# Identity matmuls placed in the planned waits of TensorE, in the attention stage of a fused attention and mixture-of-experts kernel

## The chip, the cores and the metric

The kernel runs on one core of one Trainium2 chip. The metric is the device time of one execution in microseconds (us). Lower is better. The time before is 783.3 us, the median of 3 runs (781.61 to 784.54).

## What is computed

The reference is attention with rotated queries and keys, and behind it a mixture of eight experts of which each token takes two.

```python
# q, k, v: (4, 8, 576, 64) float32
q_rot, k_rot = rotate(q), rotate(k)
scores = q_rot @ k_rot.T / sqrt(64)
attn = exp(scores - max(scores)); attn /= sum(attn) + 1e-9
x = (attn @ v)                       # as rows: (2304, 512)
noisy = x @ w_gate + log1p(exp(x @ w_noise)) * noise
top2_w = softmax of the two largest of noisy
out[token] += top2_w * (relu(x @ w1[e]) @ w2[e])   # for the two experts e of the token
```

## The kernel before

The kernel has two stages. Attention runs until about 350 us and handles 32 heads as 16 pairs. The experts run from about 356 us to the end. Between them the tokens are routed: logits, places and indirect DMAs that put each token's row into its experts' lists.

In attention each pair has nine score blocks in two passes. Pass 1 (`s1`, with keys as the moving operand) computes the scores for the row maxima. VectorE (DVE) reduces each block (`mx`, L556). Pass 2 (`s2`) computes the scores again, transposed, and takes the maximum off by a further matmul with `qlm`. ScalarE (ACT) takes the exponential (`ex`, L656), and the result is split in two 16-bit parts by DVE (L663), GpSimd (POOL, L667) or ACT (L660). Both passes contract over 64 rows, so that they use half of TensorE's rows at a time (64-row form). Then `av` multiplies the probabilities with the values and sums them up in `ACC` (128-row form).

`ACC` is one tile of PSUM with two banks of 512 columns, one for each head of the pair. The sums use columns 0 to 324 of each bank. There is one `ACC` for all pairs. When the last `av` of a pair is done, DVE normalises the sums in place (`n0` to `n2`, L751), ACT copies them out (`xh`, L772) and DVE takes the remainder out (`xl`, L770). Only then can the first `av` of the next pair write to `ACC`. The score blocks go through a ring of three other PSUM tiles (`ps`, two banks each, named `big`).

All of this is laid out by a planner within the kernel's source (`Plan`). Every step is an `Op` with an engine, a planned duration, its dependencies, a priority and the buffers that it uses. `Plan.order()` plays the steps through with these durations, and gives each one a planned begin and end. The steps are then issued in the order of their planned begins, engine by engine, and this order is fixed: an instruction that has to wait on the chip holds whatever stands behind it on its engine. TensorE (PE) and the others find each other by semaphores that the framework sets where two instructions touch the same tile; in PSUM it orders any two that touch the same bank. The planner adds `SWITCH` (.095 us) where TensorE goes from the 64-row to the 128-row form or back.

At the start, `warm` issues 24 matmuls of a 128x128 identity (`ident`) into columns 0 to 127 of `ACC` (L863). Four groups of transposes follow (L443, 5 matmuls each), and later 5 transposes of the maxima (L598). `swap_left` is the point in the plan at which attention's buffers are given up.

Of the kernel before, what the change touches and what calls it, by code (L numbers as in the profile page):

```python
# [22 lines left out]
NP = B * H // 2  # L23
# [9 lines left out]
FAR = 1 << 20  # L33

SWITCH = .095
LAG = dict(PE=.16, DVE=.05, ACT=.05, POOL=.05, SP=.05, Z=0.0)
CFG = {'T': 12.38,
 'bufP': 5,
# [116 lines left out]
class Ring:  # L155


    def __init__(self, name, bufs, make):
        self.name, self.bufs, self.make, self.taken = name, bufs, make, []


class Buf:


    def __init__(self, ring, make=None):
        self.ring, self.make, self.left, self.t, self.held = ring, make or ring.make, 0, None, False

    def __call__(self):
        if self.t is None:
            self.t = self.make()  # L170
        return self.t
# [9 lines left out]
class Plan:  # L181
# [14 lines left out]
    def order(self):  # L196
        for op in self.ops:
            for d in set(op.deps):
                p = self.by[d]
                p.out.append(op)  # L200
                op.left += 1
        now, k, port, rows = 0.0, 0, None, 128
        ready = {e: [] for e in ("PE", "DVE", "ACT", "POOL", "SP", "Z")}
        run, ev, dma, started = {}, [], 0.0, []

        def push(t, kind, op):
            nonlocal k
            k += 1
            heapq.heappush(ev, (t, k, kind, op))

        for op in self.ops:
            if op.after > 0:
                op.left += 1
                push(op.after, "start", op)
            if op.left == 0:
                ready[op.eng].append(op)

        def free(op):
            for b in op.uses:
                if b.held:  # L220
                    continue
                n = len(b.ring.taken)
                if n >= b.ring.bufs and b.ring.taken[n - b.ring.bufs].left:
                    return False
            return True

        def reach(op, same):
            for q in op.out:
                if (q.eng == op.eng and op.land is None) == same:
                    q.left -= 1  # L230
                    if q.left == 0:
                        q.rdy = now
                        ready[q.eng].append(q)

        def go():
            nonlocal port, rows
            any_ = True
            while any_:
                any_ = False
                for e, rl in ready.items():  # L240
                    if e in run or not rl:
                        continue
                    for op in sorted(rl, key=lambda o: o.prio):
                        if free(op):
                            break
                    else:
                        continue
                    rl.remove(op)
                    for b in op.uses:
                        if not b.held:  # L250
                            b.held = True
                            b.ring.taken.append(b)
                    op.begin = now
                    started.append(op)
                    run[e] = [op, op.dur]
                    if e == "PE":
                        run[e][1] += SWITCH if op.rows != rows else 0.0
                        rows = op.rows
                    any_ = True
                    if op.port and port is None:  # L260
                        port = e
                    if e == "Z":
                        finish(e)

        def finish(e):
            nonlocal dma, port
            op = run.pop(e)[0]
            op.end = now
            if port == e:
                port = next((x for x, r in run.items() if r[0].port), None)  # L270
            if op.land is not None:
                dma = max(dma, now + 0.3) + op.land
                push(dma + 1.4, "far", op)
            else:
                push(now + LAG[e], "far", op)
                reach(op, True)

        while True:
            go()
            on = [e for e, r in run.items() if not r[0].port or e == port]  # L280
            t = min([now + run[e][1] for e in on] + ([ev[0][0]] if ev else []), default=None)
            if t is None:
                break
            for e in on:
                run[e][1] -= t - now
            now = max(now, t)
            for e in [e for e, r in run.items() if r[1] < 1e-9]:
                finish(e)
            while ev and ev[0][0] <= now + 1e-9:
                _, _, kind, op = heapq.heappop(ev)  # L290
                if kind == "start":
                    op.left -= 1
                    if op.left == 0:
                        op.rdy = now
                        ready[op.eng].append(op)
                else:
                    reach(op, False)
                    for b in op.uses:
                        b.left -= 1
        stuck = [o.name for o in self.ops if o.begin is None]  # L300
        assert not stuck, (len(stuck), now, stuck[:40])
        self.span = now
        return started


def build(ctx, tc, q, k, v, w_gate, w_noise, noise, w1, w2, tab_d, out):
    nc = tc.nc
# [13 lines left out]
    plan = Plan()  # L321
# [7 lines left out]
    ACC = sml.tile([128, 2, 512], F32, name="acc")  # L329
# [8 lines left out]
    ident = cp.tile([128, 128], F16, name="ident")  # L338
# [13 lines left out]
    bigs = Ring("big", 3, lambda: big.tile([128, 1024], F32, name="ps"))  # L352
# [430 lines left out]
    def simple(name, eng, dur, fn, prio=-95.0, deps=(), **kw):  # L783
        add(name, eng, dur, fn, deps=deps, prio=prio, **kw)
# [73 lines left out]
        simple(("zero", i), "ACT", .6, lambda i=i: fill_out(i), prio=210 + 7 * i, land=1.4,  # L858
               deps=["pad"], after=210 + 7 * i)

    def warm(n):
        for _ in range(n):
            nc.tensor.matmul(ACC[:, 0, 0:128], ident, ident, start=True, stop=True)  # L863
    simple("warm", "PE", 2.4, lambda: warm(24), prio=-99, deps=["ident", ("add", "q", 0, 0)])


# [511 lines left out]
    for o, d in zip(plan.ops, CFG["dp"].split()):  # L1378
        o.prio += int(d) / 10
    todo = plan.order()  # L1380
    if CFG.get("dry"):
        return plan, todo
    for o in todo:
        for b in o.uses:
            b()
        o.fn()
    manual.close()

# [107 lines left out]
```

## Time and profile before

| what | value |
|---|---|
| median of 3 runs | 783.3 us (781.61 to 784.54) |
| profiled execution, its own time | 784.09 us |
| span of that execution, first to last instruction | 782.3 us |
| granted TensorE clock, mean over the span | 0.969 |
| TensorE (matmul) busy | 714.0 us, 91% |
| DVE, ACT, POOL busy | 410.9, 284.3, 363.5 us |

The span is what the trace shows; 1.8 us of the execution lie outside it. A granted clock of 1.00 is 2.4 GHz and 0.50 is 1.2 GHz. "Idle before" is the time in which an engine had nothing running just before an instruction, with what ended it. Matmuls are pipelined: one that takes 219 ns from start to end can start 58 ns behind the one before it.

### The profile page before, as it was taken

What the parts mean: (1) busy time and instruction counts of PE and PEld (TensorE: products, weight loads), DVE (VectorE), ACT (ScalarE), POOL (GpSimd) and SP (SyncE); (2) the same over time, 40 slices, a digit from 0 to 9 for tenths busy, and PEclk for the clock granted to TensorE, in tenths of its full rate; (3) what the DMA queues carried; (4) which work ended last, traced back from release to release, by engine and by line L of the source; (5) the groups of instructions that cost most, each with busy time, mean ns of one, the idle gap of its engine ahead of it and who ended that gap; (6) DMA issues with size and microseconds to landing.
All of it is one profiled execution on the core that took longest, in us unless ns stands there. A gap on an engine that the chain in (4) does not pass through costs nothing.

```text
span 782.3 us, 17906 instructions
## 1 busy us (share of the span) xinstructions
PE 714.0 (91%) x7736; PEld 484.7 (62%) x7736; DVE 410.9 (53%) x653; ACT 284.3 (36%) x428; POOL 363.5 (46%) x315
## 2 busy tenths in 40 slices
PE   3889878989897889889999999999999999999995
PEld 2667666777775767778655557456465574664652
DVE  6758768867858868668224515334333343342211
ACT  2543637535545555845113313213223132140100
POOL 4699797894523678744622313131330321312311
PEclk9989989989898999999999999999999999999998
DMA  7675756957726595566755697745555437441201
GB/s 154 146 155 119 144 116 140 194 90 117 131 56 147 199 177 173 148 166 214 243 153 161 124 165 204 203 128 150 175 165 163 132 114 202 129 134 54 78 28 39
DMA packets 178808, 112.09 MB, mean 143 GB/s; under 512 B 150431, under 2 KB 155039, under 8 KB 178720
## 3 DMA queue, kind: packets, MB, share of 16 engines
q1 hardware_dynamic: 161632, 72.72, 42.5%
q0 software_dynamic: 9120, 29.03, 11.0%
q10 hardware_dynamic: 7968, 9.12, 3.5%
q8 instruction: 62, 1.02, 0.5%
q14 instruction: 26, 0.21, 0.1%
HBM read 58.57 MB, written 29.22 MB: 112 GB/s over the span
## 4 chain that ended last, share of the span: by engine, by line
PE 50%; issue 12%; DVE 6%; DMA 6%; POOL 5%; ACT 3%; POOLq 0%; ACTq 0%; DVEq 0%
PE ps L531 24%; PE dn L531 18%; PE acc L531 7%; DMA prev<-out_dram,meta 3%; DMA out_dram<-y,meta 2%; POOL p L667 2%; POOL out_dram L1296 1%; POOL prev L1250 1%; DVE xr L770 1%; ACT p L656 1%; ACT xr L772 1%; DMA qlm<-tmx 1%; DVE acc L751 1%; ACT ps L656 1%; DVE nm L556 1%
## 5 line engine op out<-in xcount | busy, mean ns | idle before, releaser
L531 PE MATMUL dn<-w2h,hid 128*128 128x512 f16 x640 | 192.0, 379 | 0.0
L531 PE MATMUL ps<-xt,w1h 128*128 128x320 f16 (+2 forms) x960 | 177.6, 301 | 0.2 <-DVE hid L1223 0.2
L1296 POOL DMA_INDIRECT out_dram<-y,meta x40 | 53.3, 1332 | 247.8 <-DVE y L1289 204.0
L531 PEld LDWEIGHTS <-hid 128*128 128x128 f16 x960 | 93.9, 98 | 111.7
L667 POOL TENSOR_TENSOR p<-p 128x1152 f16<-128x1152 f32 (+1 forms) x50 | 102.4, 2060 | 61.2 <-ACT p L656 60.8
L531 PEld LDWEIGHTS <-w1h 128*128 128x128 f16 x1024 | 100.0, 98 | 41.6 <-issue 0.9
L1225 ACT ACTIVATE hid<-ps 128x640 f16<-128x640 f32 (+2 forms) x80 | 47.8, 597 | 210.9 <-PE ps L531 210.9
L531 PE MATMUL dn<-w2l,hid 128*128 128x512 f16 x320 | 121.3, 379 | 0.0
L531 PE MATMUL ps<-xt,w1l 128*128 128x320 f16 (+2 forms) x480 | 113.1, 301 | 0.0
L656 ACT ACTIVATE p<-ps,pbias 128x576 f32<-128x576 f32 x115 | 81.5, 741 | 84.6 <-PE ps L531 79.4
L556 DVE TENSOR_REDUCE nm<-ps 128x2 f32<-128x576 f32 x128 | 91.7, 751 | 33.3 <-PE ps L531 32.9
L1223 DVE SCALAR_TENSOR_TENSOR hid<-ps,hid 128x640 f16<-128x640 f32 (+2 forms) x80 | 54.8, 690 | 99.1 <-ACT hid L1225 99.1
L531 PE MATMUL ps<-qt,kt 64*128 64x288 f16 (+5 forms) x1200 | 88.4, 270 | 15.3 <-DVE p L663 4.6
L1289 DVE SCALAR_TENSOR_TENSOR y<-dn,gsc,prev 128x512 f32<-128x512 f32 x38 | 28.5, 751 | 139.9 <-PE dn L531 120.6
L531 PE MATMUL acc<-vb,p 128*128 128x65 f16 (+3 forms) x2040 | 81.7, 197 | 12.0 <-DVE xr L770 5.8
L531 PE MATMUL ps<-kt,qt 64*128 64x288 f16 (+1 forms) x960 | 83.9, 302 | 6.4 <-DVE nm L556 2.6
L531 PEld LDWEIGHTS <-p 128*128 128x128 bf16 (+3 forms) x2040 | 72.8, 100 | 26.5 <-issue 16.2
L531 PEld LDWEIGHTS <-kt 64*128 64x128 f16 (+1 forms) x1200 | 56.1, 100 | 30.6 <-issue 22.5
L531 PEld LDWEIGHTS <-qt 64*128 64x128 f16 (+1 forms) x960 | 49.1, 101 | 24.7 <-issue 14.1
L1250 POOL DMA_INDIRECT prev<-out_dram,meta x38 | 41.9, 1101 | 46.9 <-DMA out_dram<-y,meta 28.2
L531 PEld LDWEIGHTS <-w1l 128*128 128x128 f16 x512 | 50.1, 98 | 19.4
L1058 POOL DMA_INDIRECT xs_rows<-xr,r_ii x36 | 41.7, 1158 | 30.6 <-DVE r_got L1046 12.6
(136 smaller groups left out, 747.8 us busy)
## 6 DMA issues: line engine op xcount, KB each, us to landing
wst<-in_moe_w_dram SPq DMA_DIRECT2D x64, 512.0 KB, 4.2
out_dram<-pad ACTq DMA_DIRECT2D x18, 256.0 KB, 3.9
xs_rows<-pad ACTq DMA_DIRECT2D x8, 522.0 KB, 3.3
qin<-in_q_dram SPq DMA_DIRECT2D x16, 256.0 KB, 4.1
qin<-in_k_dram SPq DMA_DIRECT2D x16, 256.0 KB, 3.8
vin<-in_v_dram SPq DMA_DIRECT2D x16, 256.0 KB, 3.5
out_dram<-y,meta POOLq DMA_INDIRECT x40, 5.0
prev<-out_dram,meta POOLq DMA_INDIRECT x38, 3.8
```

What stands on the lines that cost most here:

```text
L531: nc.tensor.matmul(o, w, m, start=first, stop=last, skip_group_check=True)
L556: nc.vector.tensor_reduce(nm()[:, u, :, h], x, axis=AX.X, op=OP.max, negate=True)
L656: nc.scalar.activation(x if way[u] == "P" else halves(whole(u), u, h), x, AF.Exp, bias=pbias, scale=0.125 / (QS * QS))
L667: E.tensor_tensor(b, whole(u), a, op=OP.subtract)
L751: nc.vector.tensor_tensor(xv(), a5[:, :, :, 0:64], ri[0][:, :, :, None].to_broadcast([128, 2, 5, 64]), op=OP.mult)
L770: nc.vector.tensor_tensor(at_, xx, to, op=OP.subtract)
L1058: i = nc.gpsimd.indirect_dma_start(out=xs, out_offset=bass.IndirectOffsetOnAxis(ap=h["ii"][:, t, a:a + 1], axis=0), in_=r[:, slot(t)], in_ ...
L1223: nc.vector.scalar_tensor_tensor(hl, ps[:, 0:n, 0:w_], 0.0, hh, op0=OP.max, op1=OP.subtract)
L1225: nc.scalar.activation(hh, ps[:, 0:n, 0:w_], AF.Relu)
L1250: nc.gpsimd.indirect_dma_start(out=prev, out_offset=None, in_=out, in_offset=bass.IndirectOffsetOnAxis(ap=ids(e, j, 1), axis=0))
L1289: nc.vector.scalar_tensor_tensor(y, dn(), s["gsc"][j], s["prev"][j], op0=OP.mult, op1=OP.add)
L1296: i = nc.gpsimd.indirect_dma_start(out=out, out_offset=bass.IndirectOffsetOnAxis(ap=ids(e, j, 0), axis=0), in_=yt[0], in_offset=None, boun ...
```

## The change

TensorE gets extra matmuls of the identity with itself ("fills"), whose results nobody reads. After the planner has ordered all steps, a new passage looks at each pair of PE steps that follow each other in the plan, up to `swap_left`. A planned wait gets fills in front of the step `z` that ends it, if it is at least .3 us long, begins after `warm`, and if the planned busy share of PE is at most `LOW` (.8) in at least one of three stretches of 3.4 us around it. Their number is `FILL` (.7) of the wait less .1 us, divided by .055 us.

Where they write is chosen as follows. If the wait does not overlap a planned reading of `ACC` (from the begin of a pair's last `av` to .2 us after its last `xl`), they go to columns 384 to 511 of `ACC`'s first bank, without the start flag. Otherwise, if `z` is a score block whose `ps` tile is planned to be free by the start of the wait, they go to columns 320 to 447 of that tile, with the start flag. Otherwise there are none. `Buf` and `Plan` only note when a buffer was done with; the order of the steps is that of before. `warm` itself moves from columns 0 to 127 to columns 384 to 511.

```diff
+LOW, FILL = .8, .7
...
         self.ring, self.make, self.left, self.t, self.held = ring, make or ring.make, 0, None, False
+        self.since = self.done = 0.0
...
                             b.held = True
+                            if len(b.ring.taken) >= b.ring.bufs:
+                                b.since = b.ring.taken[-b.ring.bufs].done
                             b.ring.taken.append(b)
...
                     for b in op.uses:
                         b.left -= 1
+                        b.done = now
...
-    def warm(n):
+    def warm(n, to=None, begin=True):
         for _ in range(n):
-            nc.tensor.matmul(ACC[:, 0, 0:128], ident, ident, start=True, stop=True)
+            nc.tensor.matmul(ACC[:, 0, 384:512] if to is None else to[:, 320:448], ident, ident, start=begin, stop=True,
+                             skip_group_check=True)
...
     todo = plan.order()
+    busy = [o for o in todo if o.eng == "PE" and o.begin < plan.by["swap_left"].begin]
+    reads = [(min(plan.by["av", n, 8, j].begin for j in range(2)), max(plan.by["xl", n, m].end for m in range(2)) + .2)
+             for n in range(NP)]
+
+    def share(a, z):
+        return sum(max(0.0, min(z, o.end) - max(a, o.begin)) for o in busy if o.end > a and o.begin < z) / (z - a)
+    idle = {}
+    for a, z in zip(busy, busy[1:]):
+        gap = z.begin - a.end
+        if gap < .3 or z.begin < plan.by["warm"].end + .1:
+            continue
+        if min(share(t, t + 3.4) for t in (a.end - 3.4 + .5 * gap, a.end - 1.7 + .5 * gap, a.end - .5 * gap)) > LOW:
+            continue
+        own = [b for b in z.uses if b.ring is bigs]
+        if not any(f < z.begin and a.end < t for f, t in reads):
+            to = ()
+        elif own and z.name[0] in ("s1", "s2") and own[0].since < a.end + .1:
+            to = own
+        else:
+            continue
+        idle[z] = max(1, int(FILL * (gap - .1) / .055)), to
...
     for o in todo:
         for b in o.uses:
             b()
+        if o in idle:
+
+            warm(idle[o][0], *[b() for b in idle[o][1]], begin=bool(idle[o][1]))
         o.fn()
```

## Rows read from the trace of the kernel before

**Rows 1.** The page, part 2: busy tenths and granted clock in 40 equal slices.

```profile
PE   3889878989897889889999999999999999999995
PEclk9989989989898999999999999999999999999998
```

**Rows 2.** Windows: length, busy us (count) of PE, PEld, DVE, ACT, POOL, clock, DMA, GB/s.

```profile
20.00:350.00 330.00, 285.27 (x5091) 230.56 (x5087) 241.04 (x401) 176.13 (x282) 235.06 (x144) 0.94 0.64 142
```

**Rows 3.** Windows, the seven stretches at the lower clock ahead of the experts.

```profile
30.18:33.59 3.41, 3.41 (x54) 3.20 (x52) 2.39 (x8) 2.90 (x5) 1.47 (x1) 0.50 0.91 177
47.24:54.07 6.83, 6.30 (x83) 5.66 (x83) 2.28 (x6) 2.09 (x5) 6.75 (x4) 0.50 0.64 132
105.27:112.10 6.83, 5.49 (x70) 4.03 (x68) 2.06 (x6) 2.35 (x3) 6.75 (x3) 0.50 0.70 152
166.71:173.54 6.83, 6.83 (x56) 4.70 (x55) 2.94 (x5) 1.03 (x1) 6.83 (x4) 0.50 0.12 41
207.67:217.91 10.24, 10.24 (x85) 7.85 (x86) 5.97 (x6) 1.04 (x2) 3.29 (x2) 0.50 0.91 146
238.39:245.22 6.83, 5.57 (x68) 3.98 (x68) 6.14 (x22) 0.78 (x2) 0.80 (x1) 0.50 0.63 129
351.03:354.44 3.41, 3.41 (x33) 3.41 (x34) 3.07 (x10) 2.02 (x2) 0.00 (x0) 0.50 0.94 202
```

**Rows 4.** Timeline of PE: start, us, engine, line, form, count, [idle before <- ended by].

```profile
28.28 0.45 PE L598 MATMUL ps<-ident,tmx 128*128 128x128 f16 x5 [2.29 <-DVE tmx L583]
...
46.48 0.20 PE L531 MATMUL acc<-vb,p 128*128 128x65 f16 x1 [0.56 <-DVE p L663]
...
104.47 0.54 PE L531 MATMUL ps<-qt,kt 64*128 64x288 f16 x6 [0.83 <-ACT p L656]
...
166.49 2.22 PE L531 MATMUL acc<-vf,p 128*128 128x65 f32 x10 [2.15 <-DVE xr L770]
...
206.43 1.09 PE L531 MATMUL acc<-vb,p 128*128 128x65 f16 x30 [1.86 <-DVE xr L770]
...
239.54 0.22 PE L531 MATMUL ps<-r_sel,before 128*128 128x72 f16 x1 [3.62 <-DVE p L663]
...
332.68 4.09 PE L531 MATMUL acc<-vb,p 128*128 128x65 f16 x117 [1.30 <-POOL p L667]
...
350.98 3.64 PE L949 MATMUL ps<-ident,xr 128*128 128x128 f16 x33 [0.88 <-DVE xr L770]
```

**Rows 5.** Timeline of PE near the start.

```profile
1.39 2.74 PE L863 MATMUL acc<-ident 128*128 128x128 f16 x24 [1.39 <-POOL ident masks.py:199]
13.24 0.72 PE L443 MATMUL ps<-ident,tq 128*128 128x128 f16 x5 [9.12 <-ACT tq L425]
```

**Rows 6.** Matmuls with the identity: duration ns min/median/max, first and last start, form.

```profile
L863 PE MATMUL acc<-ident x24: 287/314/314, 1.4 to 3.8; 128*128 128x128 f16 x24
L598 PE MATMUL ps<-ident,tmx x5: 219/219/230, 28.3 to 28.5; 128*128 128x128 f16 x5
```

**Rows 7.** Windows, the first score blocks.

```profile
18.00:23.40 5.40, 4.93 (x41) 3.40 (x42) 3.67 (x6) 2.94 (x6) 4.74 (x3) 1.00 0.38 86
```

**Rows 8.** Timeline of PE, score blocks one behind the other, then `av`.

```profile
117.78 0.53 PE L531 MATMUL ps<-qt,kt 64*128 64x288 f16 x6
...
118.30 0.55 PE L531 MATMUL ps<-qt,kt 64*128 64x288 f16 x6
...
118.90 2.02 PE L531 MATMUL acc<-vb,p 128*128 128x65 f16 x60
```

**Rows 9.** Timeline of DVE, one reading of `ACC`: its first large and its last instruction.

```profile
202.24 0.84 DVE L751 TENSOR_TENSOR acc<-acc,ri 128x640 f32<-128x640 f32 x1
...
206.08 0.29 DVE L770 TENSOR_TENSOR xr<-acc,xr 64x128 f16<-64x128 f32 x1
```

**Rows 10.** The page, part 5: line, engine, form, count, busy, mean ns, idle before.

```profile
L656 ACT ACTIVATE p<-ps,pbias 128x576 f32<-128x576 f32 x115 | 81.5, 741 | 84.6 <-PE ps L531 79.4
```

**Rows 11.** Waits of PE: engine, line, ended by: us in total, times, longest.

```profile
PE acc L531 <- DVE xr L770: 8.8, 8, 2.2
```

More of the change, by code (lines that the diff above doesn't have):

```diff
@@ L1380, in build @@
     todo = plan.order()
+    busy = [o for o in todo if o.eng == "PE" and o.begin < plan.by["swap_left"].begin]
[18 more added lines that the diff above has]
+        idle[z] = max(1, int(FILL * (gap - .1) / .055)), to
     if CFG.get("dry"):
+        plan.idle = idle
         return plan, todo
```

## The prediction, made before the change was run

> **What bounds the kernel now.** I read the page's slices first: TensorE is busy in nine tenths and more of nearly every slice, and the granted clock dips in the left half only [rows 1]. So the experts run at the full clock without waits, and nothing that this change does can shorten them. What is open is attention: in the 330 us from 20 to 350 TensorE works 285.3 us and waits 44.7, while DVE works 241.0, POOL 235.1 and ACT 176.1 [rows 2]. TensorE is the busiest but not the only bound.
>
> Then I looked up each dip. Ahead of the experts there are seven stretches at half clock, together 44.4 us, in which TensorE is busy for 41.25 us [rows 3]. At full clock that work would take about half, 20.6 us less. That is the most that holding the clock can give, and only if nothing else were late.
>
> Last came the waits that end just ahead of, or inside, each stretch, because a fill can only stand where the planner sees a wait. Ahead of 30.2 it is the wait for the first maxima, 2.29 us; ahead of 47.2 a row of waits of about .56 us; ahead of 105.3 one of .83; around 238.4 one of 3.62 for the routing chain. Ahead of 166.7 and 207.7 it is an `av` that waits for `xl`, that is for the reading of `ACC` (2.15 and 1.86 us, "DVE xr"); ahead of 351.0 a transpose after `swap_left` [rows 4].
>
> **What the fills reach.** The rule bars fills into `ACC` while it is being read, and an `av` has no `ps` tile to fall back to. So the waits ahead of 166.7 and 207.7 get none, nor does the one ahead of 351.0, which is past the end of the rule. These three keep 20.5 us of half clock [rows 3]. The stretches at 30.2, 47.2, 105.3 and 238.4 are within reach. The planner's own waits stand in no view; I take the run's waits in their stead. By the rule I find 26 waits of .3 us or more outside a reading, from the one of 9.12 us before 13.24 [rows 5] to the one of 1.30 us before 332.68 [rows 4], 34.2 us in all. Seven tenths of each, at .055 us a fill, make about 390 fills: 114 in the long first wait, some 270 in the other 25.
>
> **The price of one fill.** The five transposes at 28.28 have the same shape: .45 us together [rows 4], one alone .219 [rows 6], so they start (.45 - .22)/4 = .058 us apart. `warm` took (2.74 - .31)/23 = .106 us each [rows 5, 6]. In a wait that is really there, 390 fills cost nothing: they end within seven tenths of it at .058, and the rest is slack. Where the run has no wait at that place, each costs its .058 us. The bounds are 0 and 270 x .058 = 15.7 us. The other engines' steps take longer than planned (the exponential .741 us [rows 10] against .64 in the plan), so the run's waits should be longer than the plan's more often than shorter; I take a tenth, 1.6 us. The loads of the identity are as many as the fills, and run beside them.
>
> **The form.** Fills are in the 128-row form. Between two score blocks they add two changes of form. A score block starts .52 us after the one before it, and the `av` behind the last one starts .60 after it [rows 8], so a change costs about .08 to .10 us. About a dozen of the 25 waits lie between score blocks: 12 x 2 x .10 = 2.4 us if no slack covered it, 0 if all did. The slack (three tenths of a wait) covers it from waits of .7 us on; I take 1.0. The Trainium skill ("TensorEngine Tiling (Array Packing)", Key Properties) says that a change of tiling mode "drains the TensorE". Should each change cost a whole drain of .22 us, as one transpose took alone, the item would be up to 12 x 2 x .22 = 5.3 us and the forecast four later; the .10 of the trace speaks against that.
>
> **What the clock gives back.** In the four stretches within reach TensorE is busy 3.41 + 6.30 + 5.49 + 5.57 = 20.8 us, so 10.4 us of its time could go. How much of that reaches the end depends on who else is free. In the stretches at 47.2 and 105.3 DVE and ACT work a third of the time: they wait for TensorE, and the half goes through whole, (6.30 + 5.49)/2 = 5.9. POOL is full there, but of the waits in [rows 4, 5] it ends only one, so I don't count it. At 30.2 and 238.4 DVE is busy 2.39 of 3.41 and 6.14 of 6.83 [rows 3]; no more than its idle time can go through, 1.0 and .7. Sum 7.6, bounds 0 (the others take over at once) and 10.4.
>
> **The start.** The page grants 1.00 from the first slice [rows 1], but `warm` ran at .106 us a matmul, twice the .058, and the first transposes took .72 us for five against .45 later [rows 4, 5]. So TensorE runs at half pace until some time between 13 and 28 us. With 114 fills in the wait of 9.12 us it would come to the first score blocks at full pace. From 18.0 to 23.4 it is busy 4.93 us, of which half could go, and DVE leaves 1.73 us idle there [rows 7]; it becomes the bound. I take 1.0, bounds 0 and 1.7. The Trainium skill ("TensorE: Matmul & The Clock Gate", Seeing it yourself) warns that clock events in the trace "have been observed to be unreliable"; the spacing bears that out here. By the clock column alone this item would be 0.
>
> **The new wait.** A fill writes to the bank of `ACC` that DVE and ACT read, so it waits for the reading to be really over. The plan keeps .2 us behind `xl`; in the run the part from `n2` on can take 4.1 us (from 202.24 to 206.37 [rows 9]), where its own steps add up to 2.2 in the plan (.75, .49, .2, .6 and .2). If fills stand right behind a late reading, TensorE stands at them, and behind them the next score block, then DVE's maximum and ACT's exponential. On average I take 0 for it and keep it as a rival.
>
> **The sum.** 7.6 + 1.0 - 1.6 - 1.0 = 6.0 us off the profiled execution's 784.1: 778.1. That execution lies .8 over the median of 783.3, from which it would be 777.3. I say 778.
>
> **The rivals.** *The waits are elsewhere.* The fills stand where the planner thinks TensorE waits, and the run's waits arise from DVE and ACT being late. Then one or two of the four stretches stay, or a new one comes elsewhere, and the costs are paid: between 781 and 786, say 783. For it speaks that the wait of 1.30 us ahead of 332.68 led to no dip while one of .83 stands ahead of another [rows 3, 4]: small shifts decide. Against it speaks that the order is fixed and the same chains cause the same waits.
>
> *The clock holds throughout.* If the shifted order also loses the dips at 166.7 and 207.7, (6.83 + 10.24)/2 = 8.5 us more of TensorE's time could go, at most two thirds of it through to the end: 772.
>
> *Held at the reading of `ACC`.* Fills behind a late reading stop TensorE for up to 4.1 - 2.2 = 1.9 us, ahead of score blocks that could have run. There are 16 pairs. Three held in full eat the 6 us; from five on the kernel is measurably slower; eight give 784.1 - 6 + 8 x 1.9 = 793. For it: `xr` ends eight waits of an `av` already, up to 2.2 us [rows 11]. Against it: a fill must fall in the first 1.9 us behind the planned end, and those eight waits belong to an `av`, which is barred.
>
> **How the numbers follow.** Forecast (774 to 781) .47; waits elsewhere .27; clock holds throughout .11; held at the reading .15. This kernel's measurement can't tell less than about 0.5% from no change, so faster means below 779.4 and slower above 787.2. Faster takes most of the forecast (.39) and the whole of the third case, with a little of the second: .52. Slower takes most of the fourth and the edge of the second: .15. Same: .33. The range is 768 to 787: it leaves out some .05 below and .13 above.
>
> **What would show it.** Right: the rows at 30, 47, 105 and 238 are at 1.00 and those at 166, 207 and 351 stay; new matmuls `acc<-ident` stand within waits, about 270 behind 20 us, .058 us apart, with TensorE's idle time ahead of the real steps shorter; the first score blocks run twice as fast, and the experts take as long as before and begin about 6 us earlier. Wrong step by step: a mean clock still near 0.97 means that the fills miss; a clock near 1.00 with the same time means that the others took over; a wait ahead of `acc<-ident` ended by "DVE xr" means the new wait. The prediction is off altogether if the planner sees far more waits than the run has, so that the fills number many hundreds and lengthen TensorE's queue by more than the clock gives back.

## The result and the profile after

The changed kernel takes 776.66 us, the median of 4 runs (770.53 to 777.91), against 783.92 us for the kernel before on the same footing. The ratio is 0.9897, with a 95% interval of 0.9858 to 0.9936, so about 1.0% faster. The forecast was 778. The profiled execution took 775.57 us with a span of 773.8, 8.5 us less than that of before. The same kernel took 770.53 us in a run with a mean granted clock of 0.992, and 777.91 in one with 0.978.

The page's slices of the changed kernel (busy tenths and granted clock in 40 equal slices), which answer [rows 1]:

```profile
PE   4899988989888999879999999999999999999995
PEclk7999999999899999999999999999999999999998
```

The dips in the first half are fewer. Its windows (length, busy us and count of PE, PEld, DVE, ACT, POOL, then clock, DMA, GB/s) answer [rows 2, 3]; these are all its stretches at half clock ahead of the experts, and attention as a whole:

```profile
7.95:18.18 10.23, 4.36 (x38) 3.84 (x39) 9.50 (x10) 2.14 (x3) 6.99 (x4) 0.50 0.76 145
164.97:168.37 3.40, 3.40 (x34) 2.38 (x35) 1.48 (x2) 0.45 (x1) 3.40 (x2) 0.50 0.01 3
202.52:209.33 6.81, 6.81 (x62) 5.54 (x62) 4.54 (x4) 2.25 (x3) 4.49 (x2) 0.50 0.90 200
229.82:233.22 3.40, 3.40 (x45) 2.42 (x42) 2.67 (x5) 3.27 (x6) 0.00 (x0) 0.50 0.58 112
342.45:345.86 3.41, 3.03 (x29) 3.04 (x30) 3.06 (x11) 2.13 (x4) 0.00 (x0) 0.50 1.07 254
...
20.00:350.00 330.00, 298.74 (x5528) 245.58 (x5524) 247.89 (x426) 181.04 (x291) 238.15 (x147) 0.97 0.66 150
```

Behind 20 us, 17.0 us at half clock are left of 44.4. The stretches at 30, 47 and 105 are gone, those at 166, 207 and 238 are each 3.4 us shorter, and the one behind attention is as long as before. The first row is no new stretch: there the clock column now shows what in the kernel before only the spacing of the matmuls showed, in [rows 5, 6] (the five transposes at 13 us take .72 us there and .71 here).

The fills in the timeline of PE (start, us, engine, line, form, count); 358 of them in 24 groups, of which the first two behind `warm`, both begun within the stretch at half clock, a typical one and the largest are shown:

```profile
1.39 2.74 PE L868 MATMUL acc<-ident 128*128 128x128 f16 x24 [1.39 <-POOL ident masks.py:199]
13.11 0.71 PE L448 MATMUL ps<-ident,tq 128*128 128x128 f16 x5 [8.98 <-ACT tq L430]
...
15.01 1.06 PE L868 MATMUL acc<-ident 128*128 128x128 f16 x8
16.61 1.98 PE L868 MATMUL acc<-ident 128*128 128x128 f16 x19
...
103.10 1.85 PE L868 MATMUL acc<-ident 128*128 128x128 f16 x30
...
233.33 2.40 PE L868 MATMUL acc<-ident 128*128 128x128 f16 x40
```

None has idle time ahead of it apart from `warm`, which waits for the identity itself. Forty take 2.40 us, so (2.40 - .22)/39 = .056 us each. In the first group, at half clock, they start (1.06 - .31)/7 = .107 us apart. The wait of 9 us ahead of 13.11 got no fills at all.

The waits of PE (ended by: us in total, times, longest):

```profile
PE acc L536 <- DVE xr L775: 8.8, 8, 2.1
PE ps L536 <- DVE nm L561: 3.3, 4, 1.1
PE ps L536 <- ACT p L661: 3.2, 9, 0.6
PE ps L536 <- DVE p L668: 2.5, 5, 0.8
```

The first is that of [rows 11], unchanged. The table sets the begin of a pair's normalisation (L751; L756 after) against the kernel before, in us, for the profiled executions of this kernel and of the experiments below that ran on comparable chips:

| kernel | pair 1 | 3 | 4 | 7 | 9 | 12 | 16 | span |
|---|---|---|---|---|---|---|---|---|
| changed | -1.5 | -0.5 | -2.8 | -3.9 | -5.5 | -8.6 | -8.1 | -8.5 |
| fills to 40 us only | +0.7 | +0.7 | +0.9 | +1.8 | +1.8 | 0.0 | +0.3 | +0.6 |
| fills 40 to 100 only | -2.4 | -0.6 | -1.8 | -1.7 | -3.3 | -3.9 | -3.8 | -4.3 |
| fills from 100 only | 0.0 | 0.0 | -2.2 | -3.3 | -3.3 | -7.0 | -7.2 | -7.3 |
| one fill a group | -1.7 | +0.8 | +2.2 | +2.3 | +2.3 | +1.0 | +1.0 | +0.3 |
| twice the fills | +1.9 | +7.8 | +8.0 | +9.3 | +7.8 | +4.0 | +4.5 | +3.8 |
| two groups more | -1.2 | -0.2 | -2.5 | -5.1 | -9.8 | -14.0 | -14.1 | -15.4 |

### The profile page after: what moved, and what is told of

Its sections match the earlier page's. It is cut to its first block, busy times and chain, and to the rows that moved or that the text cites. A ratio compares the mean times of both kernels' runs of the same rounds, so it can differ in the third digit from the quotient of the medians.

```text
span 773.8 us, 18622 instructions
## 1 busy us (share of the span) xinstructions
PE 722.3 (93%) x8094; PEld 495.7 (64%) x8094; DVE 411.0 (53%) x653; ACT 284.1 (37%) x428; POOL 362.4 (47%) x315
## 3 DMA queue, kind: packets, MB, share of 16 engines
q8 instruction: 65, 1.06, 0.6%
## 4 chain that ended last, share of the span: by engine, by line
PE 54%; issue 11%; DVE 8%; ACT 3%; POOL 3%; DMA 3%; SPq 0%; POOLq 0%; ACTq 0%; DVEq 0%
PE ps L536 26%; PE dn L536 20%; PE acc L536 6%; DVE nm L561 2%; POOL out_dram L1302 1%; ACT p L661 1%; DMA out_dram<-y,meta 1%; DMA prev<-out_dram,meta 1%; DVE xr L775 1%; POOL prev L1256 1%; POOL p L672 1%; ACT xr L777 1%; ACT ps L661 1%; DVE acc L756 1%; DMA gt<-xr 1%
## 5 line engine op out<-in xcount | busy, mean ns | idle before, releaser
L536 PE MATMUL ps<-qt,kt 64*128 64x288 f16 (+5 forms) x1200 | 83.9, 261 | 7.8 <-DVE p L668 2.1
L536 PE MATMUL acc<-vb,p 128*128 128x65 f16 (+3 forms) x2040 | 78.6, 195 | 8.7 <-DVE xr L775 5.8
L536 PE MATMUL ps<-kt,qt 64*128 64x288 f16 (+1 forms) x960 | 80.1, 290 | 7.1 <-DVE nm L561 2.2
L536 PEld LDWEIGHTS <-p 128*128 128x128 bf16 (+3 forms) x2040 | 70.4, 98 | 21.8 <-issue 15.5
L536 PEld LDWEIGHTS <-kt 64*128 64x128 f16 (+1 forms) x1200 | 52.3, 97 | 22.2 <-issue 13.3
L536 PEld LDWEIGHTS <-qt 64*128 64x128 f16 (+1 forms) x960 | 47.3, 98 | 23.8 <-issue 14.4
L1256 POOL DMA_INDIRECT prev<-out_dram,meta x38 | 38.9, 1023 | 45.9 <-DMA out_dram<-y,meta 27.6
```

What stands on the lines that cost most here:

```text
L536: nc.tensor.matmul(o, w, m, start=first, stop=last, skip_group_check=True)
L1256: nc.gpsimd.indirect_dma_start(out=prev, out_offset=None, in_=out, in_offset=bass.IndirectOffsetOnAxis(ap=ids(e, j, 1), axis=0))
```

## The experiments

Four questions were open: is it the clock, where do the gains lie, what does a fill cost that has no wait, and why did the early gain not last. Times are medians, ratios are to the kernel before on the same chip.

**Is it the clock? One fill in each place (`e4_one`).**

```diff
-        idle[z] = max(1, int(FILL * (gap - .1) / .055)), to
+        idle[z] = 1, to
```

> All 28 groups stay at their places with their waits, but each has one fill in place of 2 to 40. Clock theory: 28 fills keep TensorE busy for 1.6 us only, so the stretches near 30, 47, 105 and 238 are back and the time is that of before, 783 to 784. The rival that the added waits and the shifted order make the gain, not the clock: 777 as with the full change.

Measured: 783.93 us, ratio 0.9994 (0.9973 to 1.0015). The trace holds 24 single fills, so there are 24 groups and not the 28 of the expectation. The first five of its eight stretches at half clock:

```profile
29.08:32.48 3.40, 3.25 (x44) 2.84 (x45) 2.52 (x8) 2.32 (x4) 0.05 (x1) 0.50 0.80 178
49.56:52.96 3.40, 3.40 (x34) 2.05 (x35) 2.10 (x5) 1.99 (x5) 3.40 (x2) 0.50 0.48 108
83.69:87.09 3.40, 3.40 (x52) 3.13 (x51) 1.13 (x1) 2.66 (x5) 3.29 (x2) 0.50 0.75 157
104.17:114.40 10.23, 7.84 (x88) 5.17 (x84) 5.32 (x9) 3.80 (x5) 8.47 (x4) 0.50 0.50 128
169.02:175.84 6.82, 6.82 (x56) 4.70 (x56) 2.99 (x5) 1.00 (x1) 6.82 (x4) 0.50 0.11 39
```

The stretches at half clock are back, and with them the time. The places, the waits on `ACC` and the changes of form are those of the full change, so none of these makes the gain. One stretch, near 84, stands where before had none.

The single fills also mark the places in the trace, and show whether TensorE waits there. At the place where the change puts 36 fills it doesn't:

```profile
47.39 2.17 PE L536 MATMUL acc<-vb,p 128*128 128x65 f16 x55 [0.56 <-DVE p L668]
49.49 0.27 PE L868 MATMUL ps<-ident 128*128 128x128 f16 x1
49.70 0.90 PE L536 MATMUL ps<-qt,kt 64*128 64x288 f16 x6
```

The score block stands right behind the fill. The same holds for 12 of the 24 places, and in the kernel before TensorE waits less than .1 us at each of these 12. With the full change they hold 141 of the 358 fills, 7.9 us at .056.

**Where the gains lie. Fills of one part of attention alone (`e1_early`, `e2_mid`, `e3_late`).** The rule of the change is kept, with a bound on the planned begin:

```diff
-        if gap < .3 or z.begin < plan.by["warm"].end + .1:
+        if gap < .3 or z.begin < plan.by["warm"].end + .1 or z.begin > 40:   # e1_early
+        if gap < .3 or not 40 < z.begin < 100:                               # e2_mid
+        if gap < .3 or z.begin < 100:                                        # e3_late
```

> Only the six groups of fills planned before 40 us are kept (80 fills). By the theory that the time follows the stretches at half clock: no stretch at 30, those near 47 (6.8 us), 105 (6.8) and 238 (6.8) as before, and 0.5 to 2 us less than before, about 782.5. By the rival that it is the changed timing of the first score blocks which carries through to the end: most of the gain of the full change, below 779.

> Only the groups planned between 40 and 100 us are kept (some 155 fills). Clock theory: the stretch near 47 is gone, those near 30, 105 and 238 stay; the sums of the first pair come about 3 us earlier, but in the full change this lead had shrunk to 0.5 us by the third pair, so the time is within 1 us of before, 783. The rival that a freed half clock goes through whole to the end: 3 us less, 780.5.

> Only the groups planned from 100 us on are kept (some 123 fills). Clock theory: the stretches near 30 and 47 stay, those near 105 and 238 are gone or halved; 4 to 6 us less than before, 779, most of the gain of the full change. If the gain came from the early fills and was carried on, this run shows 783.

Measured: 782.74 us (ratio 0.9970, 0.9948 to 0.9992), 781.89 (0.9978, 0.9960 to 0.9995) and 776.95 (0.9903, 0.9881 to 0.9925). The fills from 100 us on, a third of all, make practically the whole gain. Those ahead of 100 us remove the stretches at 30 and 47 (the one at 30 is absent from the profile of `e2_mid` too, without fills there), but bring 0.2 to 0.3% each, and the table shows that a lead of 2.4 us at the first pair is 0.6 at the third. The expected 782.5, 783 and 779 were near for the first two; the last was undervalued by 2 us.

**What takes the early lead? The three groups ahead of the stretch at 47 alone (`e10_dip47`).** This run, and `e6_warm`, `e11_lean` and `e12_two`, were on a chip on which the kernel before took 793.9 us, so that only their ratios compare with the rest.

```diff
+        if gap < .3 or not 40 < z.begin < 52:
```

> Only the three groups of fills ahead of the stretch near 47 (planned between 40 and 52 us, 78 fills) are kept. With all groups from 40 to 100 the first pair's sums came 2.4 us early and the third's 0.6. If it is the other engines that take the lead back, it shrinks to about 0.6 here too, and the time is about 782. If the fills between 52 and 100 us, ahead of which no stretch at half clock stood, cost it (77 fills of .058 us, 4.5 us at most), the third pair's sums stay about 2 us early and the time is 1 to 2 us better than with them, 780.5.

Measured: ratio 0.9977 (0.9957 to 0.9997). The lead is 1.9 us at the first pair and 1.2 at the second, so it shrinks without the fills behind 52 us. Behind that a stretch at half clock near 83 came up, and the third pair is 0.5 us late. `e4_one` and `e12_two` have such a stretch too, the kernel before and `e11_lean` have none, so it isn't shown that the fills between 52 and 100 us keep it away. One rival is left in this run: the 36 fills without a wait are one of its three groups, and they stand between the sums of the first pair and those of the second:

```profile
49.34 2.18 PE L868 MATMUL ps<-ident 128*128 128x128 f16 x36
51.46 0.54 PE L536 MATMUL ps<-qt,kt 64*128 64x288 f16 x6
```

No run leaves out this group alone. In `e12_two`, without fills there, the lead shrinks as well (2.6 to 1.3 us), but over a stretch at half clock. The other place to look is the timeline of ACT; for the kernel before, for the fills from 40 to 100 us, and for this run:

```profile
59.83 1.16 ACT L425 CAST tq<-qin 128x1152 f16<-128x1152 f32 x1
72.74 1.15 ACT L425 CAST tq<-qin 128x1152 f16<-128x1152 f32 x1 [10.48 <-POOL qin L422]
```

```profile
58.18 1.16 ACT L430 CAST tq<-qin 128x1152 f16<-128x1152 f32 x1
72.19 1.15 ACT L430 CAST tq<-qin 128x1152 f16<-128x1152 f32 x1 [11.57 <-POOL qin L427]
```

```profile
58.66 1.16 ACT L430 CAST tq<-qin 128x1152 f16<-128x1152 f32 x1
72.34 1.15 ACT L430 CAST tq<-qin 128x1152 f16<-128x1152 f32 x1 [11.25 <-POOL qin L427]
```

The first cast comes 1.65 and 1.17 us earlier, the second only .55 and .40: ACT then stands for 11 us before POOL's rotation of the next group of heads, with everything that is queued behind it. POOL is busy without a pause there, and doesn't finish sooner because TensorE does.

**Is it POOL? Part of POOL's work taken away, without fills and with those from 40 to 100 us (`e8_cut`, `e9_cutmid`).** Both kernels leave out eight ninths of three steps of the rotation, so their results are not the reference's.

```diff
+                e = a + 1 if (d, x) in ((1, "k"), (2, "q"), (2, "k")) else z
-                t = qin()[:, a:z]...
+                t = qin()[:, a:e]...
```

> The kernel before, with three of POOL's steps in the rotation of the queries and keys (t1 for the keys of the second group of four heads, and for queries and keys of the third) cut to one ninth: that part of the rotation is left out. It is the partner of the next run, and shows how far POOL holds the pairs near 75 and 100 us: about 7 us of POOL's work less by 70 us. If POOL through ScalarE's wait for it (10.5 us, ending at 72.7) sets the pace there, the sums of the second pair come some us before 75.7.

> The same cut, with the fills planned between 40 and 100 us. In the run of those fills alone the first pair's sums came 2.4 us early and the third pair's only 0.6 us early. If the lead was given back to POOL, it now stays: the third pair's sums come 1.5 us or more ahead of those of the cut without fills. If TensorE's own waits for VectorE and ScalarE took it, it shrinks to about 0.6 us here too.

Measured: 778.24 us (ratio 0.9950, 0.9926 to 0.9973) and 782.78 (0.9991, 0.9975 to 1.0007). The pair doesn't isolate POOL's part, and what it shows speaks against POOL as the one cause. In the profiled execution without fills the stretch near 47 didn't come up at all, so that there was nothing for the fills to gain. Its first pair is 2.0 us ahead of before, and the lead stays whole to the third pair (-2.05, -2.04, -2.05). With the fills it is -0.6 at the first pair, +0.1 at the second and +0.4 at the third: the lead shrinks by 1.0 us here too, though POOL's work is cut. ACT's wait for POOL is shorter in both (8.31 us, against 10.48) and ends at 68.51 and 70.65 in place of 72.74. In the run with fills that is 2.1 us earlier than before, and the second and third pairs come no earlier for it. So the rows above show ACT's wait, and no experiment shows that it takes the lead. It stays open how much the 36 fills without a wait take and how much the waits between ACT and DVE. The run with fills takes 4.5 us longer than the one without. In the profiles, which lie 6.1 us apart, 2.4 us are there at the third pair, and most of the rest comes where the stretches near 165 and 203 are 3.4 us shorter without the fills. So the pair gives no price of a fill.

**What a fill costs without a wait. Twice the fills (`e5_double`).**

```diff
-LOW, FILL = .8, .7
+LOW, FILL = .8, 1.4
```

> The changed kernel with twice the fills in each of the 28 places (some 716 in place of 358), so that they last 1.4 times the planned wait. Prediction's price: what goes beyond the wait costs .058 us a fill. The planned waits filled add up to about 29 us; four tenths of it, 11 us, would overrun, and with a third to two thirds of it on the path the time is 4 to 8 us above the changed kernel, 781 to 785. If TensorE's queue is far from the bound in these places, it stays within 2 us, 777 to 779.

Measured: 788.15 us, ratio 1.0071 (1.0050 to 1.0092). The changed kernel on this chip would be at 783.12 x 0.9897 = 775.1, so the surplus costs 13 us. It is some 370 fills x .058 = 21.5 us of TensorE's time, of which 60% comes through on the whole. That is more than expected. The row of attention shows where the rest went:

```profile
20.00:350.00 330.00, 308.60 (x5713) 256.32 (x5711) 236.29 (x392) 176.02 (x280) 234.06 (x144) 0.97 0.62 141
```

TensorE is idle for 21.4 us of these 330, with the change for 31.3. So, as an estimate from these two rows, some 10 us of the surplus stood in waits, and the other 11 to 12 came through about whole. The clock is much the same (0.978 to 0.984 in its runs, 0.978 to 0.992 with the change), so that nothing is gained.

**The start. 150 matmuls in `warm` (`e6_warm`).**

```diff
-    simple("warm", "PE", 2.4, lambda: warm(24), ...
+    simple("warm", "PE", 2.4, lambda: warm(150), ...
```

> The changed kernel with 150 matmuls in place of 24 in the first group, which fill the wait of 9 us that the fills of the change left empty. By the prediction's term for the start: the first transposes and score blocks run at full clock and the time is 0.5 to 1.7 us less than the changed kernel's 776.7. If VectorE and POOL set the pace of the first blocks: the first score blocks at full clock, and no difference, within 0.5 us.

Measured: ratio 0.9891 (0.9856 to 0.9927), against 0.9897 of the change. The timeline of PE:

```profile
1.39 10.13 PE L868 MATMUL acc<-ident 128*128 128x128 f16 x150 [1.39 <-POOL ident masks.py:199]
13.07 0.45 PE L448 MATMUL ps<-ident,tq 128*128 128x128 f16 x5 [1.55 <-ACT tq L430]
14.46 0.45 PE L448 MATMUL ps<-ident,tq 128*128 128x128 f16 x5 [0.94 <-ACT tq L430]
...
19.04 3.49 PE L536 MATMUL ps<-kt,qt 64*128 64x288 f16 x36
```

The transposes take .45 us in place of .71, but they begin when ACT and DVE let them, at 13.07 (13.11 with the change). The first score block begins at 19.04 (19.30), and the first pair's sums come .2 us later than with the change. But the start isn't wholly at full clock: the next stretch is at half.

```profile
14.99:18.40 3.41, 3.41 (x36) 3.41 (x34) 2.25 (x4) 0.69 (x1) 2.85 (x2) 0.50 0.87 159
```

So a filled first wait brings nothing clear of the noise, and what a start at full clock all through would bring isn't shown.

**The waits that the rule bars. Two groups more (`e7_ahead`), and these two alone (`e12_two`, with `if gap < 1e6` in place of the rule's condition, so that it places none).** One stands ahead of the `av` that waits for `xl` near 164 us and writes to the `ps` tile of the score block that follows, which is free there; the other ahead of the first transpose behind attention, into that transpose's own tile.

```diff
+    for nm, own, gap in ((("av", 6, 0, 1), None, 2.0), (("r", 2, "turn", 0), ("r", 2, "turn", 0), 2.3)):
+        z = plan.by[nm]
+        own = plan.by[own] if own else next(o for o in todo[todo.index(z) + 1:] if o.eng == "PE" and any(b.ring is bigs for b in o.uses))
+        idle[z] = int(FILL * (gap - .1) / .055), [b for b in own.uses if b.ring is bigs]
```

> The changed kernel with 24 fills more ahead of the seventh pair's first matmul with the values (the wait near 164 us for the reading of the sums), written to the free tile of the next score block, and 28 more ahead of the first transpose behind attention (the wait near 341 us). Clock theory: the stretches at half clock near 165 (3.4 us) and 342 (3.4 us) go as well, and 1 to 3 us come off the 776.7. If these waits are on the path whatever the clock does, the stretches go and the time stays within 0.5 us of 776.7.

> The kernel before with the two added groups alone: 24 fills ahead of the seventh pair's first matmul with the values, 28 ahead of the first transpose behind attention. Clock theory: the stretches near 30, 47, 105 and 238 as before, those near 167 and 351 gone; the 7.9 us by which the two groups improved the changed kernel come partly from the stretch near 207, which has no fill of its own and moved; so here 2 to 5 us less than before, 779 to 781. If the two groups bring their 8 us whatever stands ahead of them: 775.

Measured: 768.75 us (ratio 0.9821, 0.9798 to 0.9843) on top of the change, and a ratio of 0.9908 (0.9875 to 0.9941) alone. Cores, windows and timeline of the first:

```profile
core 0: 766.9 us, clock 0.998
```

```profile
20.00:350.00 330.00, 301.33 (x5645) 248.86 (x5643) 254.15 (x452) 185.45 (x300) 239.07 (x151) 1.00 0.69 152
```

```profile
162.16 1.50 PE L868 MATMUL ps<-ident 128*128 128x128 f16 x24
164.46 1.33 PE L536 MATMUL acc<-vf,p 128*128 128x65 f32 x10 [0.81 <-DVE xr L775]
...
201.31 1.09 PE L536 MATMUL acc<-vb,p 128*128 128x65 f16 x30 [1.86 <-DVE xr L775]
```

In this execution the clock never falls within attention. The fills take 1.50 us of the wait and leave .81, so the `av` is not held. The wait of 1.86 near 201 has no fills and is as long as in [rows 4], but the clock holds behind it: what the two groups did to the stretch near 202 is an effect of the shift, not of fills in its place. The changed kernel on this chip would be at 775.1, so the two groups bring 6.3 us, two to six times what was expected for the two stretches at 165 and 342. For the two groups alone (7 us by the ratio) the gain lies near the second of the two expectations. The gains of both changes about add up (1.0, 0.9 and together 1.8%). This version beats both kernels. The stretches at half clock of the two groups alone:

```profile
47.98:54.81 6.83, 6.32 (x67) 4.48 (x66) 2.85 (x6) 3.75 (x7) 6.75 (x4) 0.50 0.92 181
82.11:85.52 3.41, 3.41 (x41) 2.57 (x36) 2.24 (x3) 2.66 (x5) 2.34 (x1) 0.50 0.74 138
102.59:109.42 6.83, 6.00 (x64) 4.17 (x63) 3.18 (x7) 2.01 (x3) 6.75 (x3) 0.50 0.84 179
232.30:235.71 3.41, 3.18 (x43) 2.40 (x44) 3.30 (x15) 0.26 (x1) 0.00 (x0) 0.50 0.71 147
242.54:249.37 6.83, 5.87 (x80) 4.54 (x81) 5.53 (x13) 4.28 (x6) 4.55 (x5) 0.50 0.67 123
```

Those at 166, 207 and 351 are gone, and so is the one at 30, though no fills stand there; one near 82 is new. In all 27.3 us at half clock are left of 44.4. This execution is the fastest of its seven (779.94, the median is 787.41), so the others may have more.

**Without the fills between 52 and 100 us (`e11_lean`).** The kernel with the two added groups, less the groups in that stretch:

```diff
+        if gap < .3 or z.begin < plan.by["warm"].end + .1 or 52 < z.begin < 100:
```

> The kernel with the two added groups (768.75), without the groups planned between 52 and 100 us. If those cost without giving, 1 to 2 us less, 767. If they hold the clock in stretches that would otherwise fall, some us more, 770 to 772.

Measured: ratio 0.9856 (0.9824 to 0.9888), which overlaps 0.9821 (0.9798 to 0.9843) a little. So nothing is won by leaving them out, and some of the clock may be lost; the runs don't tell how much.

## Why the prediction came out right, step by step

**The bound** held, though not by the first reading: nine tenths in nearly every slice of [rows 1] is true of the experts, while 13 of the 18 slices of attention show less. [rows 2] has the waits of attention right. The gain lies in attention alone: 8.4 of the 8.5 us are there when the first expert's second matrix begins, and TensorE's granted clock is what changed.

**Which stretches the fills reach** was right for those at 30, 47 and 105, which went, for the one at 238, which was halved, and for the one behind attention, which stayed. Those at 166 and 207 stayed too, as said, but each was shorter by 3.4 us. That was not forecast, and it is a share of the gain: pair 7 gains 1.6 us more than pair 6 on it, pair 9 gains 1.5 more than pair 8.

**The number and the price of the fills.** The price was right, .056 us each against .058. The number came near by luck, 358 fills against 390. The 114 fills for the first wait don't exist: the planner lets `warm` wait for the first rotation, so in the plan it runs late and has no wait behind it, while on the chip it runs at 1.39. I had read the wait from the trace and not the plan's `deps`. And behind 20 us there are 322 fills where I had 270. The step that failed is "I take the run's waits in their stead", with "the run's waits should be longer than the plan's more often than shorter": by the single fills of `e4_one`, 12 of the 24 places have no wait to speak of. The term for missing waits was 1.6 us; the fills in these 12 places alone take 7.9 us of TensorE's time. How much of it reached the end isn't measured.

**The start** (1.0 us) had its fills from that wait, and `e6_warm` shows no gain clear of the noise from filling it. The first maxima's transposes do begin earlier with the change (27.44 against 28.28), but with the same early fills in `e1_early` they begin at 28.75, and in `e10_dip47`, which has none there, at 27.62. So this lead isn't shown to be the fills'. The clock column says 1.00 from 0 to 8 us in both kernels while `warm` runs at .106 us a matmul. The warning of the Trainium skill ("TensorE: Matmul & The Clock Gate", Seeing it yourself) that clock events in a trace have been unreliable is borne out by that.

**What the clock gives back** was near in the sum and wrong in its parts. For the stretches at 30 and 47 I had taken 4.1 us; the third pair is 0.5 us ahead. For 105 it was 2.7, and the fourth pair gains 2.3. For 238 it was 0.7, and pairs 9 to 11 gain 0.9. The step that failed is that at 47.2 "the half goes through whole": a lead is there at the first pair (1.5 us) and shrinks to 0.5 by the third. Why stays open. POOL, which I didn't count, ends a wait of ACT's that is 10.5 us long; but `e9_cutmid`, where that wait ends 2.1 us earlier, doesn't bear out that it sets the pace, and the 36 fills without a wait are a rival. On the other side, a further 2.3 us come between pairs 11 and 12, which no term holds. There DVE's split of a weight chunk runs beside POOL's split of `p`; the kernel before, then the changed one, DVE and POOL:

```profile
272.83 3.02 DVE L1124 SCALAR_TENSOR_TENSOR w1l<-wst,w1h 128x1024 f16<-128x1024 f32 x1
272.66 2.11 POOL L667 TENSOR_TENSOR p<-p 128x1152 f16<-128x1152 f32 x1 [1.62 <-ACT p L656]
```

```profile
266.49 1.22 DVE L1130 SCALAR_TENSOR_TENSOR w1l<-wst,w1h 128x1024 f16<-128x1024 f32 x1
266.88 2.79 POOL L672 TENSOR_TENSOR p<-p 128x1152 f16<-128x1152 f32 x1 [2.19 <-ACT p L661]
```

Before, POOL began .17 us ahead of DVE, and DVE's operation took 3.02 us; after, DVE began .39 ahead and took 1.22, and POOL paid .68. So the order of the two begins, which the shift changed, goes with 1.8 us of DVE's time. That it makes the 2.3 us is argued only in part: in `e3_late`, where DVE also comes first (1.22 us), these two pairs gain 2.3 as well, but in `e1_early`, `e2_mid` and `e4_one`, where POOL comes first (3.02 to 3.08 us), they still gain .8 to .9. So of the 8.5 us some 3.7 belong to the terms that I had (105, 238 and the little that stays of 30 and 47), 3.1 to the stretches that I had left out, and the rest mostly to this. These leads hold the price of the fills already. That the sum of 6.0 came near 8.5 is thus partly luck: less than half of the 8.5 came from the terms that I had.

**The new wait** at the reading of `ACC` didn't come: no fill has idle time ahead of it. **The form and the missing waits** (2.6 us) were not measured alone. `e5_double` says that the value rested on the waits being there: of its surplus, what found no wait came through about whole.

Of the rivals, the one in which the waits lie elsewhere was right in its premise for half of the places, and wrong in its time (783): three of the four stretches went all the same. The one in which the clock holds throughout needed the two further groups, and gave 768.75 there, below its 772.

## What to carry to other kernels

Where TensorE's granted clock falls behind short waits, matmuls that nobody reads keep it up, if they fit into the wait and into a tile that is free; look for a later step's tile where the obvious one is being read. Price the gain stretch by stretch: a freed microsecond passed through for the most part behind 100 us, and little of it between the first pair and the third. A fill in a wait that isn't there costs up to its whole time, so check that the plan's waits are the chip's. One fill in each place shows it in the trace; here half of the places had no wait.

## What the runs showed of the hardware

- The granted clock fell without one long wait: around the begin of the stretch at 47.2 us there were five waits of .28 to .56 us, ahead of 105.3 waits of .8 to 1.1. A wait alone doesn't decide: one of 1.86 us led to a fall at 207.7 in the kernel before, and one of the same length near 201 in `e7_ahead` led to none.
- The clock of the same kernel differs from run to run (0.978 to 0.992 for the changed kernel, 777.9 to 770.5 us). So a single profile shows one of several patterns, and small differences between two profiles are to be read with care.
- DVE's split of 128x1024 took 1.22 us when it began .39 us before POOL's operation and 3.02 us when it began .17 us behind it.

The five waits around 47 us in the kernel before:

```profile
44.74 0.54 PE L531 MATMUL ps<-qt,kt 64*128 64x288 f16 x6 [0.54 <-DVE nm L556]
45.69 0.23 PE L531 MATMUL acc<-vb,p 128*128 128x65 f16 x2 [0.28 <-ACT p L660]
46.48 0.20 PE L531 MATMUL acc<-vb,p 128*128 128x65 f16 x1 [0.56 <-DVE p L663]
46.98 0.23 PE L531 MATMUL acc<-vb,p 128*128 128x65 f16 x2 [0.29 <-ACT p L660]
47.77 1.44 PE L531 MATMUL acc<-vb,p 128*128 128x65 f16 x21 [0.56 <-DVE p L663]
```
